# Maxima over partitions by products of ones, the table of exponentials first, first weights by halves, a new order

## The chip, the cores and the metric

The kernel runs on one NeuronCore of a Trainium2 chip. Its engines work side by side, each through its own queue in order: TensorE (PE, with its weight loads PEld), VectorE (DVE), ScalarE (ACT), GpSimd (POOL) and SyncE (SP), which here issues nearly all DMAs. The metric is device time in microseconds of one execution, lower is better.

## What is computed

Eight sequences of 576 positions go through attention with 8 heads of 64 and then through a feed-forward layer of width 2048 with a gate. Four heads see the last 32 positions, four see every fourth of the last 128.

```python
scores = scale * np.matmul(q, k.transpose(0, 1, 3, 2))
mask_plain = (rel >= 0) & (rel < window)                       # window = 32, heads 0 to 3
mask_dil = (rel >= 0) & (rel < window * dilation) & (rel % dilation == 0)   # dilation = 4, heads 4 to 7
scores = np.where(masks[None, :, :, :], scores, -1000000000.0)
attn = np.exp(scores - np.max(scores, axis=-1, keepdims=True))
attn = attn / (np.sum(attn, axis=-1, keepdims=True) + 1e-09)
x = np.matmul(attn, v)        # then (B, S, H * D)
h = x @ w_in
sp = np.where(h > 20.0, h, np.log1p(np.exp(np.minimum(h, 20.0))))
out = (h * np.tanh(sp)) @ w_out
```

The weights come as 64-bit floats, queries, keys and values as 32-bit floats.

## The kernel before

**Units.** The work is cut into 16 units u, half a sequence (288 positions) each. A unit passes through the attention of its four pairs of heads (pairs 0 and 1 plain, 2 and 3 dilated, whose positions are grouped by residue) and then through the feed-forward layer in four column groups j of 512.

**Numbers in two halves.** The feed-forward products run in float16 with each operand split into a high part and the rest (x, w, g), so one product becomes three. A split needs a scale, a power of two taken from the operand's largest magnitude. For the weights, `w_max`, `w_words`, `w_scale` and `w_split` turn the words of a 64-bit float into a float32 and split it; the maximum over partitions comes from a bf16 product with a matrix of ones (L349, L352), a sum over partitions, which is an upper bound of the maximum. A weight piece of 1 MB (two transfers of 512 KB, named wl k.g.p: which of w_in and w_out, group, half) goes through `w_max` on ACT (L338), a shift on DVE (L381) and two word steps on DVE (L383, L384) before the scale (L349 to L362) and the split (L393 on ACT, L396 on DVE). Four pieces have room at a time.

**`prep`** takes the maxima of a unit. Units 0 to 3 ("direct") do their attention in float32 and need only the maximum of v; unit 0 ("summed") takes sums of magnitudes by ACT (L461). Units 4 to 15 need maxima of q, k and v, reduced by DVE along the free axis (L291) into a tile m of 6 columns. Over the partitions they are joined in two ways:

- `over_partitions` (units 0 to 5): PE transposes m (L300), DVE reduces (L303) and, for six columns, spreads the result on a diagonal (L306), and a float32 product with ones (L309) brings it back to all partitions;
- from unit 6 on `partition_all_reduce` on POOL (L491).

DVE reads the result (L471, L494) and makes the scales from it (L285 to L287).

**What sets the order.** A text, `ORDER`, lists steps by name; each mention of a step lets its generator run up to the next `yield` and so issues that much to the engines' queues. A number behind = names the PSUM bank (there are four, "b") that the step takes. The names are: `ld`, `lv` loads of q and k and of v, `sp` score products (L594 for the mask, L597), `sc` their row maxima on DVE (L627), `ex` exponentials (for unit 0 PE subtracts the maxima, L649), `tp` transposes of probabilities (L716, copied by ACT L725), `va` products with v (L739 or L745, L753, L759, L760), `tx` transposes of x and their split (L787, L797, L800, L802), `ff` the first feed-forward product (L841) and Mish (L844), `gt` the gate's split, `fo` the second product (L872) and the output, `wl`, `wm`, `ww`, `ws`, `wp` the weights' steps, `pr` the steps of `prep`. `kw` followed by a number issues so many products of zeros (L901), the fillers; nobody reads them.

**The first instructions** stand outside the order: the identity and the masks are made by POOL (memsets, then selects; the identity's at masks.py:199), and ACT makes bf16 copies of both (L251, L253), which every score product of the direct units reads.

Of the kernel before, what the change touches and what calls it, by code (L numbers as in the profile page):

```python
# [42 lines left out]
wp0.0.0 wp0.0.0 kw16=0 kw8=0 va0.3=0 va0.3 tp0.0=3 tp0.0 va0.3 ex1.0 wp0.3.1 wl0.1.0 wm0.1.0 ww0.1.0 ww0.1.0 wl0.2.1
xa0 kw16=3 kw7=3 tx0.2=3 va0.0=1 tx0.2 kw15=2 tp1.0=2 kw16=0 kw10=0 tx0.2 tx0.2 tp1.0 va0.0 va0.0 tx0.3=0 kw13=3
va0.1=3 va0.1 tx0.3 va0.1 wl0.2.0 kw16=2 kw5=2 tx0.3 wm0.2.0 tx0.3 ex1.1 kw14=2 tx0.1=2 tx0.1 tx0.0=1 sp1.2=3 pr1
kw11=0 tx0.1 tx0.0 sp1.3=0 tx0.0 ww0.2.0 wl0.1.1 wm0.1.1 tx0.1 wm0.2.1 sc1.2 tx0.0 kw9=2 tp1.1=2 tp1.1 ex1.2 ww0.1.1
sc1.3 ex1.3 ww0.2.1 kw4=3 ws0.1=3 ws0.1 wp0.1.0 ld2 sp2.0=1 sc2.0 ex2.0 lv2 ws0.2=2 ws0.2 fs0 kw1=3 ff0.6=3 ff0.6
ff0.6 ff0.0=0 ff0.7=2 ff0.7 ww0.2.1 ff0.7 wp0.2.1 ww0.1.1 pr1=1 pr1 ff0.0 ff0.0 pr1 pr1 va1.0=3 va1.0 va1.0 va1.1=2
va1.1 va1.1 tp1.3=1 tp1.3 tp2.0=0 tp2.0 kw2=3 tx1.0=3 va1.3=1 va1.3 tx1.0 wp0.2.1 va1.3 pr2 tp1.2=2 tp1.2 wp0.1.1
wp0.1.1 tx1.1=0 tx1.1 tx1.1 kw12=2 va1.2=2 va1.2 va1.2 tx1.0 tx1.0 wp0.1.0 gt0.3=0 ff0.1=1 ff0.1 pr2=3 ff0.1 pr2 kw1=0  # L50
tx1.3=0 tx1.3 ww0.2.0 kw10=1 tx1.2=1 tx1.2 sp2.3=2 sc2.3 tx1.3 tx1.3 kw4=0 pr2 pr2 tx1.2 tx1.2 wl1.3.0 wm1.3.0 gt0.0=1
gt0.0 ww1.3.0 wp0.2.0 wp0.2.0 ww1.3.0 wl1.3.1 wm1.3.1 ww1.3.1 ww1.3.1 fs1 kw3=0 ff1.0=0 ff1.0 ff1.0 ff1.1=1 ff1.1
ff1.1 gt1.0=2 ff1.2=3 ff1.2 ff1.2 ff1.3=0 sp2.1=1 sc2.1 ws1.3=3 ws1.3 ff1.3 ex2.3 kw6=2 tp2.3=2 tp2.3 gt0.3 gt1.0
wl1.2.0 wm1.2.0 ww1.2.0 ww1.2.0 wl1.2.1 wm1.2.1 ww1.2.1 ww1.2.1 ex2.1 kw3=3 ff0.2=3 ff0.2 ff0.2 ff0.3=2 ff0.3 ff0.3
gt0.1=3 gt0.1 ff1.6=1 ff1.6 ws1.2=3 ff0.4=2 ff1.6 ws1.2 ff1.3 gt1.1=4 gt1.1 wp1.3.0 wp1.3.0 ff0.4 va2.3=1 ff0.4
tp2.1=0 tp2.1 va2.3 va2.3 wp1.2.1 wp1.2.1 ld3 sp3.0=3 sp3.1=2 lv3 sc3.0 sc3.1 ff1.7=0 ff1.7 ff1.7 gt1.3=5 gt1.3
wp1.2.0 wp1.2.0 wp1.3.1 wp1.3.1 wl1.0.1 wm1.0.1 ff1.4=1 ff1.5=0 ff1.5 ww1.0.1 ff1.4 ff1.4 ff1.5 gt1.2=6 gt1.2 wl1.0.0
wm1.0.0 ww1.0.0 ww1.0.0 va2.1=3 va2.1 va2.1 sp3.3=2 ff0.5=1 ff0.5 ff0.5 gt0.2=7 gt0.2 fo1.2.0=0 fo1.2.1 fo1.2.2
ws1.0=1 ws1.0 ex3.1 tp3.1=3 tp3.1 wl1.1.0 wm1.1.0 fo1.2.3 fo1.2.3 fo1.2.3 sc3.3 ex3.3 sp3.2=3 sc3.2 ex3.2 ww1.1.0
ww1.1.0 sp2.2=1 ld4 sc2.2 pr4 pr4 ex2.2 lv4 fo1.3.0 fo1.3.1 fo1.3.2 fo1.3.3 fo1.3.3 pr3 fo0.2.0=2 fo0.2.1 fo0.2.2  # L60
fo0.2.3 fs2 fo0.2.3 fo0.2.3 pr4 pr4 xa2 tx2.3=3 tx2.3 tx2.3 va2.0=1 tp2.2=0 tp2.2 va2.0 va2.0 wp1.0.0 ex3.0 wp1.0.0
fo0.3.0 fo0.3.1 fo0.3.2 fo0.3.3 fo0.3.3 pr4=0 ww1.0.1 fo1.3.3 pr4 fo0.3.3 tx2.0=3 va2.2=1 tx2.0 va2.2 tx2.0 kw2=2 pr4
# [897 lines left out]
```

## Time and profile before

| | |
|---|---|
| median of three runs | 922.4 us (921.63 to 923.58) |
| the profiled execution | 923.0 us, its span 921.1 us |
| granted TensorE clock | 1.00 of full speed |
| busy, of the span | PE 99%, weight loads 80%, DVE 64%, ACT 59%, POOL 2% |
| instructions of PE | 9422 products, 482 of them fillers |
| moved by DMA | 82.36 MB, 89 GB/s on average |

PE's busy time counts a product from its start to its modelled end, so fillers count as busy like any other. Idle time is written in brackets behind an instruction, with what ended it: "<-ACT pp" is a wait for ACT's writing of pp, "<-issue" is time for which the profile shows no reason. A row with xN is a group of N instructions.

### The profile page before, as it was taken

The page shows a single profiled execution, that of the slowest core. Times are in us where ns is not written, and L with a number is a line of the kernel's source. Part 1 is how long each engine was busy: PE and PEld are TensorE (multiplying, and loading weights), DVE is VectorE, ACT ScalarE, POOL GpSimd, SP SyncE. Part 2 cuts the span into 40 slices and gives each one's busy share as a digit, 9 for nine tenths or more (in the row PEclk, how much of TensorE's full clock was granted, in tenths as well). Part 3 has the DMA queues.
Part 4 walks back from the last instruction along what each step waited for, and adds up shares of the span by engine and source line. Part 5 has one row for each costly group of instructions (what it writes and reads, how often), then busy time and mean ns, then how long its engine had stood idle before and what let it go on. Part 6 is the DMA issues. An engine that isn't in the chain of part 4 may idle for free.

```text
span 921.1 us, 21816 instructions
## 1 busy us (share of the span) xinstructions
PE 911.5 (99%) x9422; PEld 738.0 (80%) x9422; DVE 593.1 (64%) x879; ACT 545.5 (59%) x804; POOL 22.0 (2%) x99
## 2 busy tenths in 40 slices
PE   9999999999999999999999999999999999999998
...
GB/s 292 217 117 139 140 139 105 56 105 16 119 81 110 69 106 95 98 62 103 102 100 96 100 72 113 72 55 120 52 33 119 87 55 59 36 41 35 20 14 27
DMA packets 156560, 82.36 MB, mean 89 GB/s; under 512 B 122960, under 2 KB 152368, under 8 KB 156464
## 3 DMA queue, kind: packets, MB, share of 16 engines
...
q8 instruction: 74, 1.21, 0.5%
...
## 4 chain that ended last, share of the span: by engine, by line
PE 99%; ACT 1%; issue 0%; DVE 0%; ACTq 0%
PE b L872 41%; PE b L841 41%; PE b L597 4%; PE b L745 3%; PE b L901 3%; PE b L739 2%; PE b L716 1%; PE b L594 1%; PE b L649 0%; PE b L352 0%; PE b L349 0%; PE b L800 0%; PE b L787 0%; ACT pp L725 0%; PE b L309 0%; ACT x L802 0%
## 5 line engine op out<-in xcount | busy, mean ns | idle before, releaser
L872 PE MATMUL b<-g,w 128*128 128x288 f16 x3072 | 388.1, 287 | 0.0
L841 PE MATMUL b<-x,w 128*128 128x288 f16 x3072 | 387.3, 286 | 0.0
L841 PEld LDWEIGHTS <-w 128*128 128x128 f16 x3072 | 297.6, 98 | 75.3
L872 PEld LDWEIGHTS <-w 128*128 128x128 f16 x3072 | 297.1, 98 | 75.4
L862 DVE SCALAR_TENSOR_TENSOR g<-hm,sg,g 128x1152 f16<-128x1152 f32 x64 | 89.8, 1414 | 116.8 <-ACT g L860 116.8
L844 ACT ACTIVATE hm<-b,fs 128x576 f32<-128x576 f32 x128 | 92.3, 737 | 102.4 <-PE b L841 88.4
L886 ACT ACTIVATE y<-b,fo 128x288 f32<-128x288 f32 x60 | 43.5, 724 | 126.6 <-PE b L872 116.5
L860 ACT ACTIVATE g<-hm,sg 128x1152 f16<-128x1152 f32 x64 | 79.9, 1253 | 3.2 <-PE b L872 1.6
L668 ACT ACTIVATE sb<-sb,ln_p 96x704 f32<-96x704 f32 (+3 forms) x48 | 42.4, 888 | 26.8 <-DVE sb L629 26.6
L629 DVE TENSOR_TENSOR sb<-sb,nm 72x576 f32<-72x576 f32 (+4 forms) x60 | 45.2, 754 | 2.1
L627 DVE TENSOR_REDUCE nm<-sb 72x8 f32<-72x576 f32 (+4 forms) x60 | 44.9, 748 | 1.7
L760 DVE TENSOR_TENSOR xs<-b,rec 72x512 f32<-72x512 f32 (+1 forms) x64 | 39.7, 620 | 6.5 <-DVE rec L759 0.5
...
L901 PE MATMUL b<-zeros 128*128 128x128 f16 x482 | 33.4, 229 | 5.1 <-ACT pp L725 2.1
L901 PEld LDWEIGHTS <-zeros 128*128 128x128 f16 x482 | 31.0, 103 | 7.3 <-issue 5.0
L759 DVE RECIPROCAL rec<-den 72x8 f32<-72x8 f32 (+1 forms) x64 | 12.0, 188 | 36.2 <-ACT den L755 27.3
L844 ACT ACT_TABLE_LOAD x22 | 28.2, 1283 | 9.1 <-PE b L841 8.7
L621 DVE SCALAR_TENSOR_TENSOR sb<-b,sc,m_r 96x704 f32<-96x704 f32 (+1 forms) x24 | 23.4, 976 | 15.3 <-PE b L597 6.3
L597 PEld LDWEIGHTS <-q 64*72 64x72 f16 (+1 forms) x1008 | 25.8, 116 | 8.3 <-issue 7.6
L597 PE MATMUL b<-k,q 64*72 64x72 f16 (+3 forms) x1008 | 30.9, 210 | 0.0
L621 DVE SCALAR_TENSOR_TENSOR sb<-b,sc,m_d 72x576 f32<-72x576 f32 (+1 forms) x24 | 22.6, 944 | 11.4 <-PE b L597 11.0
L521 DVE TENSOR_TENSOR q<-qn,q 128x288 f16<-128x288 f32 (+1 forms) x36 | 23.7, 708 | 7.2 <-ACT q L512 7.2
...
## 6 DMA issues: line engine op xcount, KB each, us to landing
qn<-in_qT SPq DMA_DIRECT2D x16, 576.0 KB
...
raw<-in_w_in SPq DMA_DIRECT2D x16, 512.0 KB
raw<-in_w_out SPq DMA_DIRECT2D x16, 512.0 KB
...
```

The lines of the kernel that those rows point to most:

```text
L597: nc.tensor.matmul(o, q, k, start=start, stop=stop, skip_group_check=True)
L621: nc.vector.scalar_tensor_tensor(args[0], args[1], d["sc"][:nq], args[2], ALU.mult, ALU.add)
L627: nc.vector.tensor_reduce(nm[:nq, :, j:j + n], x, axis=AX.X, op=ALU.max, negate=True)
L629: nc.vector.tensor_tensor(blocked(sb, c0, n, w), x, nm[:nq, :, j:j + n].unsqueeze(3).broadcast_to([nq, 2, n, w]), op=ALU.add)
L668: nc.scalar.activation(x, x, AF.Exp, bias=ln_p[:nq])
L841: nc.tensor.matmul(ph[:, h, :HT], w1[j][:, c, wi, k * P:(k + 1) * P], x_of(d, xi, c), start=(n == 0), stop=(n == len(seq) - 1))
L844: nc.scalar.activation(d["m"][j][:, k0:k0 + 2], ph[:, :, :HT], AF.Mish, scale=d["fs"][:, j:j + 1])
L860: nc.scalar.activation(g[:, 0], m, AF.Identity, scale=sg)
L862: nc.vector.scalar_tensor_tensor(g[:, 1], m, sg, g[:, 0], ALU.mult, ALU.subtract)
L872: nc.tensor.matmul(po[:, :HT], w2[:, e, j, wi, k * P:(k + 1) * P], d["g"][j][:, gi, k, :], start=(j == 0 and n == 0), stop=(j == NCH - 1 a ...
L886: nc.scalar.activation(o, src, AF.Identity, scale=fo)
L901: nc.tensor.matmul(warm[:, 1, 512 - P:], zeros, zeros, start=True, stop=True)
```

## The change

- `over_partitions` is now one bf16 product of a matrix of ones with the maxima, which m holds as bf16: a sum over partitions in place of the maximum, in all units from 1 to 15. The all-reduce on POOL is gone. Unit 0 keeps the transpose, the reduction and the float32 product under the name `top_of`.
- In `prep` of the direct units the two reductions over v stand in separate steps.
- At the very start, before the identity, ACT takes an exponential of a column of ones.
- For the first weight piece (0.3.0) `w_max` and `w_words` work on its two 512 KB blocks one after the other (`pieces`, `BY_BLOCK`).
- `ORDER` is another one. Fillers: 120 in place of 226 ahead of the first scores, 84 in place of 212 from there to the first feed-forward product, none in place of 44 after it. The steps of the first units, and of most later ones, stand in a new order, with other banks. The weight pieces and the loads of units are asked for in the same sequence.

```diff
 ORDER = """
-wl0.3.0 wl0.0.1 ld0 wm0.3.0 ww0.3.0 ww0.3.0 wm0.0.1 ww0.0.1 ww0.0.1 kw16=0 kw16=0 kw16=0 kw16=0 kw16=0 kw16=0 kw16=0
-kw16=0 kw16=0 kw16=0 kw16=0 kw16=0 kw16=0 kw16=0 kw2=0 sp0.0=0 sc0.0 sp0.1=1 sc0.1 wl0.0.0 wm0.0.0 ww0.0.0 sp0.3=2
-wl0.3.1 wm0.3.1 sp0.2=3 sc0.2 ex0.1 ex0.1 ex0.2 ex0.2 sc0.3 ex0.3 ww0.3.1 ww0.3.1 kw2=1 ws0.3=1 ws0.3 lv0 pr0 pr0
-kw16=3 kw16=3 kw7=3 pr0=3 pr0 ww0.0.0 wp0.3.0 tp0.2=1 xa1 ex0.3 ex0.0 tp0.2 pr0 pr0 tp0.1=2 tp0.1 ws0.0=1 ws0.0
...
+wl0.3.0 wl0.0.1 ld0 wm0.3.0 wm0.3.0 ww0.3.0 ww0.3.0 ww0.3.0 ww0.3.0 wm0.0.1 ww0.0.1 ww0.0.1 kw16=0 kw16=0 kw10=0
+kw16=0 kw16=0 kw16=0 kw16=0 kw14=0
+sp0.0=0 sc0.0 sp0.1=1 sc0.1 wl0.0.0 wm0.0.0 ww0.0.0 sp0.3=2 wl0.3.1 wm0.3.1 sp0.2=3 sc0.2 ex0.1 ex0.1 ex0.2 ex0.2
+sc0.3 ex0.3 ww0.3.1 ww0.3.1 ws0.3=1 lv0 pr0 pr0 ws0.3 kw16=3 kw8=3 pr0=3 pr0 ww0.0.0 wp0.3.0 tp0.2=1 ex0.0 xa1 ex0.3
...
@@
+BY_BLOCK = {(0, 3, 0)}
+
@@
+    ones = const.tile([P, 1], F32, name="ones")
+    nc.vector.memset(ones, 1.0)
+    warm = const.tile([P, 1], F32, name="warm")
+    nc.scalar.activation(warm, ones, AF.Exp)
     ident = const.tile([P, P], F32, name="ident")
     make_identity(nc, ident)
@@
     def over_partitions(m, n):
 
+        o = take("b", banks)[:, 0, :n]
+        nc.tensor.matmul(o, ones_b.broadcast_to([P, P]), m, start=True, stop=True)
+        yield
+        return o
+
+    def top_of(m, n):
+
         pm = take("b", banks)[:, 0]
-        nc.tensor.transpose(pm[:n, :P], m, ident)
-        yield
-        c = small.tile([8, 1], F32, name="c", bufs=4)
-        nc.vector.tensor_reduce(c[:n], pm[:n, :P], axis=AX.X, op=ALU.max)
-        if n > 1:
-            dg = small.tile([8, 8], F32, name="dg", bufs=2)
-            nc.vector.tensor_scalar(dg[:n, :n], ident[:n, :n], c[:n], None, ALU.mult)
-        yield
-        o = pm[:, 256:256 + n]
-        nc.tensor.matmul(o, ones[:n].broadcast_to([n, P]), dg[:n, :n] if n > 1 else c[:n], start=True, stop=True)
+        nc.tensor.transpose(pm[:1, :P], m, ident)
+        yield
+        c = small.tile([1, 1], F32, name="c", bufs=2)
+        nc.vector.tensor_reduce(c, pm[:1, :P], axis=AX.X, op=ALU.max)
+        yield
+        o = pm[:, 256:257]
+        nc.tensor.matmul(o, ones[:1].broadcast_to([1, P]), c, start=True, stop=True)
         yield
         return o
@@
+    def pieces(k, g, p):
+        return [slice(c, c + 1) for c in range(WIDE)] if (k, g, p) in BY_BLOCK else [slice(0, WIDE)]
+
     def w_max(k, g, p):
 
         _, hi = raws[k, g, p]
         a = w_dst(k, g, p).rearrange("p c a n -> p c (a n)").bitcast(F32)
-        nc.scalar.activation(a, hi.bitcast(F32), AF.Identity, scale=HI)
+        for c in pieces(k, g, p):
+            nc.scalar.activation(a[:, c], hi[:, c].bitcast(F32), AF.Identity, scale=HI)
+            yield
@@
-        nc.vector.tensor_scalar(a, a, 3, None, ALU.logical_shift_left)
-        yield
-        nc.vector.scalar_tensor_tensor(lo, lo, 29, a, ALU.logical_shift_right, ALU.bitwise_or)
-        nc.vector.scalar_tensor_tensor(lo, hi, -0x80000000, lo, ALU.bitwise_and, ALU.bitwise_or)
+        for c in pieces(k, g, p):
+            nc.vector.tensor_scalar(a[:, c], a[:, c], 3, None, ALU.logical_shift_left)
+            yield
+            nc.vector.scalar_tensor_tensor(lo[:, c], lo[:, c], 29, a[:, c], ALU.logical_shift_right, ALU.bitwise_or)
+            nc.vector.scalar_tensor_tensor(lo[:, c], hi[:, c], -0x80000000, lo[:, c], ALU.bitwise_and, ALU.bitwise_or)
+            yield
@@
-        m = pool.tile([P, 6], F32, name="m", bufs=3)
+        m = None if u in SUMMED else pool.tile([P, 6], BF16, name="m", bufs=3)
@@
-            o = yield from over_partitions(m[:, 0:1], 1)
+            o = yield from (top_of if u in SUMMED else over_partitions)(m[:, 0:1], 1)
@@
-        if u < FIRST + 3:
-            mr = yield from over_partitions(m, 6)
-        else:
-            mr = pool.tile([P, 6], F32, name="mru", bufs=2)
-            nc.gpsimd.partition_all_reduce(mr, m, P, bass_isa.ReduceOp.absmax)
-            yield
+        mr = yield from over_partitions(m, 6)
```

More of the change, by code (lines that the diff above doesn't have):

```diff
@@ L43 @@
[L43 to L62, printed above, removed]
@@ new lines @@
+sp2.3=2 sc2.3 tx1.3 tx1.3 pr2 tx1.2 tx1.2 wl1.3.0 wm1.3.0 ww1.3.0 gt0.0=1 gt0.0 wp0.2.0 wp0.2.0 ww1.3.0 wl1.3.1
+wm1.3.1 ww1.3.1 ww1.3.1 fs1 ff1.0=0 ff1.0 ff1.0 ff1.1=3 ff1.1 ff1.1 gt1.0=2 ff1.2=1 ff1.2 ff1.2 ff1.3=0 sp2.1=3
+ws1.3=1 ws1.3 ff1.3 sc2.1 ex2.3 tp2.3=1 tp2.3 gt0.3 gt1.0 wl1.2.0 wm1.2.0 ww1.2.0 ww1.2.0 wl1.2.1 wm1.2.1 ww1.2.1
+ww1.2.1 ex2.1 ff0.2=2 ff0.2 ff0.2 ff0.3=1 ff0.3 ff0.3 gt0.1=3 gt0.1 ff1.6=3 ff1.6 ff0.4=2 ws1.2=1 ff1.6 ws1.2 wp1.3.0
+ff1.3 gt1.1=4 gt1.1 ff0.4 ff0.4 va2.3=3 tp2.1=0 tp2.1 va2.3 va2.3 wp1.2.1 wp1.2.1 wp1.3.0 ld3 sp3.0=1 sp3.1=2 lv3
@@ new lines @@
+va4.3 va4.3 ex4.0 tp4.0=0 tp4.0 tp4.0=0 fo3.2.1 fo3.2.2 fo3.2.3 sc5.2 va4.1 va4.1 sp6.1=1 sc6.1 sp5.0=2 fo3.2.3
+fo3.3.0 xa4 tx4.1=1 tx4.1 va4.0=0 tx4.1 tx4.3=0 tx4.3 va4.2=1 va4.2 va4.0 va4.0 va4.2 tx4.3 ex5.2 tp5.2=2 tp5.2
+tp5.2=2 sc5.0 fo3.2.3 ex5.3 tp5.3=1 tp5.3 tp5.3=0 tx4.2=1 tx4.0=0 tx4.0 tx4.0 tx4.2 tx4.2 fo3.3.1 fo3.3.2 fo3.3.3
+fo3.3.3 fo3.3.3 sp6.3=0 sc6.3 fo3.0.0=1 fo3.0.1 fo3.0.2 fo3.0.3 fo3.0.3 va5.2=2 va5.2 sp6.2=3 va5.2 fo3.1.0 fo3.1.1
+va5.3=0 tp5.1=0 tp5.1 sc6.2 tp5.1=1 ex5.0 tp5.0=2 tp5.0 tp5.0=2 va5.3 va5.3 fo3.0.3 pr6 pr6 lv7 ex6.1 tp6.1=1 tp6.1
@@ new lines @@
+fo5.3.2 va7.1=0 va7.1 va7.1 tp8.0=1 tx7.1=0 tx7.1 tx7.1 fo5.3.3 fo5.3.3 pr9 pr9 gt6.0=2 fo5.1.1 fo5.1.2 fo5.1.3
+fo5.1.3 tp8.1=0 xa8 va7.0=2 va7.0 va7.0 tp8.3=0 ld10 pr10 ff6.6=0 ff6.6 ff6.6 pr10 pr10 gt6.0 va7.3=1 va7.3 va7.3
+tx7.0=1 tx7.0 tx7.0 pr9 pr9 ff6.4=3 ff6.5=2 ff6.5 ff6.5 lv10 fo5.3.3 ff6.4 ff6.4 gt6.2=0 gt6.2 tx7.3=0 va8.0=0 va8.0
+ff6.7=2 ff6.7 ff6.7 gt6.3=3 gt6.3 fo6.0.0=3 fo5.1.3 sp8.2=1 sc8.2 ex8.2 fo6.2.0=2 fo6.0.1 fo6.0.2 fo6.0.3 fo6.0.3
+tp8.1 fo6.0.3 tp8.1=2 sp9.2=1 fo6.2.1 fo6.2.2 sc9.2 tp8.2=2 tp8.2 sp9.1=1 sc9.1 tp8.2=1 fo6.2.3 fo6.1.0 fo6.1.1
@@ new lines @@
+fo8.3.3 fo8.3.3 fo8.3.3 ex11.3 tx9.3 va10.3=1 tp10.2=2 va10.3 va10.3 tx9.3 tx10.3=0 tx10.3 va10.0=2 va10.0 va10.0
+tp11.2 tp11.2=0 pr12 pr12 pr12 pr12 fo8.1.0 fo8.1.1 fo8.1.2 fo8.1.3 fo8.2.3 tx10.3 sp11.0=0 sc11.0 ex11.0 tp11.0=0
+tp11.0 fo8.1.3 fo8.1.3 ff9.2=1 ff9.3=2 ff9.3 ff9.3 ff9.2 ff9.2 gt9.1=0 gt9.1 ff9.6=0 ff9.7=3 ff9.7 ff9.7 va10.1=2
+va10.1 va10.1 tp11.0=1 ff9.6 ff9.6 tx10.0=1 tx10.0 tx10.0 va10.2=1 va10.2 va10.2 pr12 pr12 pr12 ld13 pr13 lv13
+tx10.2=0 tx10.2 va11.2=3 va11.2 va11.2 ff9.0=0 ff9.1=2 ff9.1 ff9.1 ff9.0 ff9.0 gt9.0=4 gt9.0 sp12.2=1 sc12.2 xa11
@@ L166 @@
+fo14.3.3 fo14.3.3 ff15.4 gt15.2=4 gt15.2 ff15.6=2 ff15.6 ff15.6 fo13.3.3 fo13.3.3 fo13.3.3 ff15.1=0 ff15.1 ff15.1
+gt15.0=2 gt15.0 ff15.3=3 ff15.3 ff15.3 gt15.1=1 gt15.1 ff15.7=2 ff15.7 ff15.7 gt15.3=3 gt15.3 fo15.2.0=1 fo15.0.0=0
+fo15.0.1 fo15.2.1 fo15.2.2 fo15.2.3 fo15.2.3 fo15.0.2 fo15.0.3 fo15.0.3 fo15.3.0 fo15.3.1 fo15.3.2 fo15.2.3 fo15.3.3
+fo15.3.3 fo15.0.3 fo15.3.3 fo15.1.0 fo15.1.1 fo15.1.2 fo15.1.3 fo15.1.3 fo15.1.3
 """.split()
```

206 lines of the change are left out of this document (100 added, 106 removed).

## The prediction

> **What bounds the kernel now.** I read the page first, then stages, then the stages that are not full of useful work, instruction by instruction.
>
> ```profile
> span 921.1 us, 21816 instructions
> PE 911.5 (99%) x9422; PEld 738.0 (80%) x9422; DVE 593.1 (64%) x879; ACT 545.5 (59%) x804; POOL 22.0 (2%) x99
> PE 99%; ACT 1%; issue 0%; DVE 0%; ACTq 0%
> L901 PE MATMUL b<-zeros 128*128 128x128 f16 x482 | 33.4, 229 | 5.1 <-ACT pp L725 2.1
> ```
>
> PE carries the chain from end to end, but 482 of its products multiply zeros (L901, the fillers, "kw" in the order). Table by stages (length, then busy time of PE, weight load, DVE, ACT, POOL; clock; DMA), all instructions, then the fillers alone:
>
> ```profile
> 1.04:16.29 15.25, 15.25 (x228) 15.22 (x228) 5.06 (x5) 4.34 (x6) 2.34 (x12) 1.00 0.96 336
> 16.29:25.00 8.71, 8.71 (x90) 5.86 (x88) 8.05 (x12) 5.01 (x7) 0.00 (x0) 1.00 1.01 262
> 25.00:59.27 34.27, 32.04 (x426) 27.32 (x424) 28.86 (x55) 24.36 (x48) 0.24 (x2) 1.00 0.71 204
> 59.27:160.80 101.53, 99.71 (x976) 81.67 (x974) 85.47 (x143) 70.53 (x131) 0.27 (x3) 1.00 0.38 118
> 160.80:896.00 735.20, 735.20 (x7548) 591.77 (x7546) 464.86 (x665) 438.20 (x611) 18.65 (x77) 1.00 0.33 75
> 896.00:921.10 25.10, 20.57 (x168) 16.18 (x166) 0.57 (x1) 3.10 (x4) 0.00 (x0) 1.00 0.07 25
> ...
> 1.04:16.29 15.25, 15.25 (x226) 15.08 (x226) 1.00 0.96 336
> ...
> 25.00:59.27 34.27, 13.60 (x211) 12.41 (x208) 1.00 0.71 204
> 59.27:160.80 101.53, 3.87 (x44) 3.04 (x43) 1.00 0.38 118
> ```
>
> From 160.80 to 896.00 PE never waits and has no filler to speak of: only a change of its own work counts there. All that can be won lies before 160.80: the fillers, and PE's waits of 34.27 - 32.04 = 2.23 us and 101.53 - 99.71 = 1.82 us. The tail after the last product stays.
>
> The start, in order of time (start, length, engine, line; in brackets the idle time before and what ended it):
>
> ```profile
> 6.08 1.28 ACT L338 ACT_TABLE_LOAD   x1 [6.08 <-DMA raw<-in_w_in]
> 7.37 1.15 ACT L338 ACTIVATE w<-raw 128x1024 f32<-128x1024 f32 x1
> 12.47 0.28 POOL masks.py:199 TENSOR_SCALAR_AFFINE_SELECT ident<-ident 128x128 f32<-128x128 f32 x1 [11.21 <-issue]
> 12.79 0.27 ACT L253 CAST ident_b<-ident 96x96 bf16<-96x96 f32 x1 [4.27 <-POOL ident masks.py:199]
> 13.18 1.13 ACT L338 ACTIVATE w<-raw 128x1024 f32<-128x1024 f32 x1
> 14.21 0.48 ACT L251 ACTIVATE m_fb<-m_f 96x352 bf16<-96x352 f32 x1
> 14.34 0.86 DVE L381 TENSOR_SCALAR w<-w 128x1024 int32<-128x1024 int32 x1 [2.58 <-ACT w L338]
> 16.34 1.18 ACT L338 ACTIVATE w<-raw 128x1024 f32<-128x1024 f32 x1 [1.64 <-DMA raw<-in_w_in]
> 19.02 1.16 ACT L338 ACTIVATE w<-raw 128x1024 f32<-128x1024 f32 x1 [1.51 <-DMA raw<-in_w_in]
> 20.70 1.42 DVE L627 TENSOR_REDUCE nm<-b 72x8 f32<-72x576 f32 x2 [0.52 <-PE b L597]
> 22.04 0.68 DVE L381 TENSOR_SCALAR w<-w 128x1024 int32<-128x1024 int32 x1
> 24.01 1.23 DVE L384 SCALAR_TENSOR_TENSOR raw<-raw 128x1024 int32<-128x1024 int32 x1
> ```
>
> Two things hold the start. POOL stands still for 11.21 us before its first select, with no instruction and no wait that the profile knows; the mask m_fb follows only at 14.69, and 226 fillers cover that. Behind it the DMA is full (0.96, then 1.01), and the third and fourth weight pieces come when it delivers them, at 16.34 and 19.02.
>
> **The change, part by part.** *Fillers.* Counted in the two order texts: 226 become 120 ahead of the first scores, 212 become 84 from there to the first feed-forward product, 44 become none after it; 278 fewer. Whether a filler's time comes back depends on who is late next, so each stage is asked by itself.
>
> *To 25 us.* The last all-reduce by POOL is removed. Nothing on the page says that the 11.21 us belong to it; yet the select that ends them takes 0.28 us, and beside memsets and copies POOL has but two kinds of work, selects at the start and all-reduces to the end. [...] The bounds are 0 (the stall stays) and 11.21 us (it goes); I take that it goes. The first weights by halves and the table load of 1.28 us moved ahead to idle time let ACT begin when the first half has come, before 6.08, instead of at 7.37, and ident_b no longer holds ACT for 4.27 us and with it DVE for 2.58. The first scores then wait for their keys:
>
> ```profile
> qn<-in_qT SPq DMA_DIRECT2D x16, 576.0 KB
> ...
> raw<-in_w_in SPq DMA_DIRECT2D x16, 512.0 KB
> ...
> knp<-in_kT SPq DMA_DIRECT2D x8, 288.0 KB
> ```
>
> Four weight transfers, the queries and the keys of the plain heads are 2.98 MB; at 336 GB/s that is 8.9 us, so they come at 9.9 us or somewhat later, near the end of 120 fillers (1.04 + 120 x 15.25/226 = 9.1 us). But none of this moves the fourth weight piece: ACT takes it at 19.02 in any case and ends at 20.18. Before, DVE then had the maxima of two score pairs (20.70 to 22.12) ahead of that piece's shift at 22.04 and ended its last word at 25.24. With the scores some 5 us earlier these maxima are over before 20.2, so the shift starts at 20.2: 1.8 us gained of the 7.2 us of fillers taken out. Bounds 0 and 3.
>
> *From 25 us to the first feed-forward product (59.27).*
>
> ```profile
> 26.66:57.33 30.67, 28.44 (x380) 24.52 (x377) 25.54 (x44) 21.57 (x38) 0.24 (x2) 1.00 0.72 215
> ...
> 42.64 0.83 ACT L797 CAST x<-b 128x288 f16<-128x288 f32 x1
> ...
> 44.15 1.62 PE L901 MATMUL b<-zeros 128*128 128x128 f16 x26
> ...
> 45.60 0.42 PE L800 MATMUL b<-x,minus 128*128 128x288 f16 x1
> ...
> 46.06 0.79 ACT L802 CAST x<-b 128x288 f16<-128x288 f32 x1 [2.58 <-PE b L800]
> ```
>
> The fillers here are not only padding of waits. The operand of the product at 45.60 was ready at 43.47; PE was busy with 26 fillers, and ACT waited 2.58 us for PE. So taking fillers out gains, until the next engine binds: 128 fillers at 13.60/211 = 64 ns are 8.2 us, which leaves PE some 24 us of the stage, while DVE has 25.54 us of work in 30.67. The same maxima, words and products remain for DVE, so the gain ends at its idle 5.13 us. Chains from PE over ACT to DVE and back remain; I take half, 2.5 us. Bounds 0 and 5.1.
>
> *From there to 160.80.* All 44 fillers go: 3.87 us. DVE has 85.47 of 101.53 us, so PE stays the bound; I count the fillers whole and leave the 1.82 us of waits as they are: 3.9 us. Bounds 0 and 5.7.
>
> *The maxima.* Rows of the old way on PE, of a product with the same stationary ones, of POOL's way, and of the reductions ahead of it:
>
> ```profile
> 27.01 0.27 PE L300 MATMUL b<-ident,m 128*1 128x128 f32 x1
> ...
> 28.95 0.38 PE L309 MATMUL b<-c,ones 1*128 1x1 f32 x2
> ...
> L491 POOL PARTITION_ALL_REDUCE mru<-m  x10 | 4.9, 486 | 311.4 <-DVE m L291 311.4
> ...
> L349 PEld LDWEIGHTS <-ones 128*128 128x128 bf16 x16 | 1.4, 97 | 1.1
> ...
> L291 DVE TENSOR_REDUCE m<-vn 128x1 f32<-128x768 f32 x15 | 14.1, 941 | 3.9 <-DMA vn<-in_v 3.9
> ...
> L291 DVE TENSOR_REDUCE m<-vdn 72x1 f32<-72x1024 f32 x7 | 8.5, 1208 | 1.6 <-DMA vdn<-in_vd 1.6
> ```
>
> Units 1 to 5 lose a transpose and a pair of float32 products (at most 0.27 + 0.38 = 0.65 us of PE each, at least the 0.38) and ten units lose an all-reduce of 0.49 us that cost PE nothing. All 15 get one bf16 product whose weight load is the 97 ns of L349; its few columns add little: 15 x 0.1 = 1.5 us against 5 x 0.4 = 2.0. Net 0.5 us gained, bounds 1.0 lost and 1.8 gained. POOL's memset of m stays, off the path.
>
> **Sum**, against the profiled execution's own time of 923.0 (span 921.1 and 1.9 around it): 923.0 - 1.8 - 2.5 - 3.9 - 0.5 = 914.3. That execution is 0.6 above the median of 922.4, so **913.7** for the median. All good ends together are 15.6 us (906.8), all poor ends a loss of 1.0; for this case by itself I take 907 to 919, the poor end being the fillers of the last stage alone, less 0.5.
>
> [...]
>
> **The rivals.** **A, every filler counts.** PE bears the chain, others wait for it, and its own waits inside the stages are 4.05 us only, so the 278 may be pure surplus: 7.2 + 8.2 + 3.9 + 0.5 = 19.8, so 903.2, or 902.6 as a median. Against: 19.02, and 25.54 us of DVE. **B, the stall stays.** The masks come at 14.69 as before, PE idles from 9.1, the maxima sit ahead of the shift again; only 2.5 + 3.9 + 0.5 remain: 915.5. For it: nothing in the trace ties the stall to the all-reduce. **D, the stall stays and PE's clock drops** in those 5.6 us: if the stage from 16.29 to 25.00 ran at half speed, 8.7 us more, 924.2. Against: all rows show clock 1.00; for: fillers kept every wait of PE short, so the trace cannot show it. [...]
>
> **C, slower: PE queues behind the maxima.** Before, units 6 to 15 had their maxima joined on POOL, which waited 311.4 us for DVE at nobody's cost. Now the joining product stands in PE's own queue, and all feed-forward products of other units queue behind it. If PE reaches it while the last two reductions still run (0.94 + 1.21 = 2.15 us) in each of units 4 to 15, that is 12 x 2.15 = 25.8 us: 939.5. It decides from 8.7/12 = 0.7 us per unit on. Against: DVE has 464.86 of 735.20 us there, so the reductions mostly run ahead of PE.
>
> **Chances.** Forecast 48%, A 17%, B 17%, D 5%, C 9%, and 4% that the new order loses elsewhere what it gains. The range holds the forecast's own, B and A: 902.5 to 920. Within 0.2% (1.8 us) is what a measurement of this kernel can't tell from no change. Faster: forecast, A, B and a rest of D and the last, 84%; same 6%; slower, C and half of D and of the last, 10%.
>
> **What would show it.** Right: POOL's first select before 2 us; first scores at 10 to 12 us; ACT's fourth weight piece still at 19.0; the first feed-forward product at about 55; DVE over 85% busy between 25 and 55; no wait of PE after 160 us; clock 1.00. Wrong: the first select near 12.5 (B, D); the first feed-forward product before 50 (A); PE waiting at the joining product after 160 us (C); or a wait of the first FFN stage that grows by what the fillers gave.

## The result, and the profile after

The changed kernel takes 914.29 us (median of 6 runs, 913.15 to 918.24), the kernel before, on the same chip, 922.06 (6 runs, 921.12 to 924.22): a ratio of 0.9917, 95% interval 0.9895 to 0.9939. Forecast were 913.7 and a range of 902.5 to 920. The profiled execution of the changed kernel took 913.45 us, its span 911.3.

The head of its page, and the chain that ended last (the granted clock in tenths; each digit is a fortieth of the span):

```profile
span 911.3 us, 21239 instructions
PE 897.5 (98%) x9144; PEld 723.6 (79%) x9144; DVE 590.1 (65%) x875; ACT 548.1 (60%) x808; POOL 17.3 (2%) x89
PEclk9899999999999999999999999999999999999999
PE 92%; DMA 3%; DVE 2%; ACT 1%; SPq 1%; issue 1%; DVEq 0%; ACTq 0%
```

278 products fewer on PE, as many as the fillers left out, and an 8 in the second slice of the clock, where the kernel before had nines throughout. PE is now 92% of the chain: DMA and VectorE have entered it.

The stages of the changed kernel, cut at its own first feed-forward product (53.80), and under them both kernels from their first feed-forward product to the end. Columns: length, busy time of PE, weight load, DVE, ACT, POOL, granted clock, DMA share, GB/s. The changed kernel first:

```profile
25.00:53.80 28.80, 25.84 (x268) 21.09 (x267) 26.01 (x46) 23.05 (x45) 0.24 (x2) 0.88 0.84 249
53.80:155.33 101.53, 100.20 (x968) 82.00 (x967) 87.10 (x154) 73.41 (x138) 0.27 (x3) 1.00 0.42 128
155.33:886.20 730.87, 730.15 (x7504) 587.25 (x7503) 460.42 (x649) 438.38 (x608) 13.95 (x67) 1.00 0.35 74
886.20:911.30 25.10, 21.36 (x175) 16.82 (x172) 1.36 (x1) 3.09 (x4) 0.00 (x0) 1.00 0.07 24
...
53.80:911.30 857.50, 851.71 (x8642) 686.06 (x8640) 548.88 (x803) 514.88 (x749) 14.21 (x70) 1.00 0.35 79
```

and the kernel before:

```profile
59.27:921.10 861.83, 855.49 (x8686) 689.62 (x8684) 550.90 (x807) 511.82 (x746) 18.93 (x80) 1.00 0.33 79
```

So the 9.8 us between the spans split in two: 59.27 - 53.80 = 5.47 us ahead of the first feed-forward product, 861.83 - 857.50 = 4.33 us behind it. The four terms of the sum had 1.8 + 2.5 = 4.3 and 3.9 + 0.5 = 4.4. The two profiled executions flatter the change: the one before lies above its median, the one after below, and the medians differ by 7.8 us only (6.9 in a second measurement, e10). The 8.7 us of the sum is somewhat more than either. Between 25 us and that product DVE is busy for 90% (26.01 of 28.80) and the clock is 0.88.

The start of the changed kernel, in order of time:

```profile
0.73 1.28 ACT L238 ACT_TABLE_LOAD   x1 [0.73 <-PEq L962]
1.30 0.29 POOL masks.py:199 TENSOR_SCALAR_AFFINE_SELECT ident<-ident 128x128 f32<-128x128 f32 x1
4.87 0.69 ACT L351 ACTIVATE w<-raw 128x512 f32<-128x512 f32 x1 [2.64 <-DMA raw<-in_w_in]
10.12 0.50 ACT L256 ACTIVATE m_fb<-m_f 96x352 bf16<-96x352 f32 x1
12.88 0.85 PE L610 MATMUL b<-knp,qn 64*96 64x128 f32 x12 [1.75 <-DMA knp<-in_kT]
19.18 1.12 ACT L351 ACTIVATE w<-raw 128x1024 f32<-128x1024 f32 x1 [1.53 <-DMA raw<-in_w_in]
20.33 0.69 DVE L396 TENSOR_SCALAR w<-w 128x1024 int32<-128x1024 int32 x1 [0.63 <-ACT w L351]
22.32 1.23 DVE L399 SCALAR_TENSOR_TENSOR raw<-raw 128x1024 int32<-128x1024 int32 x1
```

POOL's first select stands at 1.30 us, with nothing ahead of it: the 11.21 us have gone. The fourth weight piece is still taken at 19.18 (19.02 before), its shift on DVE begins at 20.33 instead of 22.04, its last word step ends at 23.55 instead of 25.24. The first scores wait 1.75 us for their keys.

What was not foreseen stands on PE a little later. Instructions of PE, and two stretches with the columns of the stages:

```profile
33.47 1.25 PE L752 MATMUL b<-vdn,pp 72*72 72x65 f32 x16 [0.93 <-ACT pp L738]
36.40 0.71 PE L800 MATMUL b<-ident,xs 72*128 72x72 f32 x4 [1.17 <-ACT sb L675]
39.77 2.44 PE L914 MATMUL b<-zeros 128*128 128x128 f16 x21
44.41 0.67 PE L914 MATMUL b<-zeros 128*128 128x128 f16 x9
...
32.35:35.76 3.41, 1.95 (x26) 1.58 (x23) 3.24 (x7) 3.22 (x7) 0.00 (x0) 0.96 0.90 305
35.76:42.59 6.83, 6.19 (x48) 6.16 (x48) 6.66 (x9) 3.75 (x11) 0.00 (x0) 0.52 0.92 313
```

At 39.77 a filler takes 2.44/21 = 116 ns, at 44.41 it takes 74: PE ran at half clock for 6.83 us, after 3.41 us in which it was busy for 57%, though no single wait there was longer than 1.17 us. (The last section has these two stretches with the exact moments at which the clock changes.)

### The profile page after: what moved, and what is told of

The parts are those of the page before. It is cut to its first block, busy times and chain, and to the rows that moved or that the text cites. A ratio compares the mean times of both kernels' runs of the same rounds, so it can differ in the third digit from the quotient of the medians.

```text
span 911.3 us, 21239 instructions
## 1 busy us (share of the span) xinstructions
PE 897.5 (98%) x9144; PEld 723.6 (79%) x9144; DVE 590.1 (65%) x875; ACT 548.1 (60%) x808; POOL 17.3 (2%) x89
## 4 chain that ended last, share of the span: by engine, by line
PE 92%; DMA 3%; DVE 2%; ACT 1%; SPq 1%; issue 1%; DVEq 0%; ACTq 0%
PE b L885 41%; PE b L854 39%; PE b L610 4%; PE b L758 3%; DMA raw<-in_w_in 2%; PE b L752 1%; PE b L729 1%; DMA knd<-in_kdT 1%; PE b L914 0%; DVE m L296 0%; PE b L366 0%; SPq L332 0%; ACT w L409 0%; PE b L607 0%; DMA vdn<-in_vd 0%
## 5 line engine op out<-in xcount | busy, mean ns | idle before, releaser
L681 ACT ACTIVATE sb<-sb,ln_p 72x576 f32<-72x576 f32 (+3 forms) x48 | 42.5, 889 | 24.0 <-DVE sb L642 23.8
L642 DVE TENSOR_TENSOR sb<-sb,nm 96x512 f32<-96x512 f32 (+4 forms) x60 | 45.2, 754 | 2.1
L640 DVE TENSOR_REDUCE nm<-sb 96x4 f32<-96x512 f32 (+4 forms) x60 | 44.9, 748 | 1.6
L719 DVE TENSOR_TENSOR p<-sb,p 72x576 f16<-72x576 f32 (+3 forms) x34 | 30.2, 887 | 9.4 <-ACT p L717 9.4
L610 PE MATMUL b<-k,q 64*96 64x128 f16 (+3 forms) x1008 | 31.3, 210 | 0.0
L717 ACT CAST p<-sb 72x576 f16<-72x576 f32 (+3 forms) x34 | 26.5, 781 | 0.7
L351 ACT ACTIVATE w<-raw 128x1024 f32<-128x1024 f32 (+1 forms) x17 | 18.6, 1101 | 12.6 <-DMA raw<-in_w_in 12.6
```

What stands on the lines that cost most here:

```text
L610: nc.tensor.matmul(o, q, k, start=start, stop=stop, skip_group_check=True)
L640: nc.vector.tensor_reduce(nm[:nq, :, j:j + n], x, axis=AX.X, op=ALU.max, negate=True)
L642: nc.vector.tensor_tensor(blocked(sb, c0, n, w), x, nm[:nq, :, j:j + n].unsqueeze(3).broadcast_to([nq, 2, n, w]), op=ALU.add)
L681: nc.scalar.activation(x, x, AF.Exp, bias=ln_p[:nq])
```

## The experiments

The theory after the result: the stall belongs to the all-reduce; ahead of the first feed-forward product the gain is whatever VectorE and the DMA leave of the fillers taken out; behind it each filler comes back; and fillers do a second thing, they hold PE's clock (0.88 between 25 us and that product in the changed kernel, 1.00 in the kernel before). Rivals: the stall alone was the cost; the fillers were surplus everywhere; the halves and the early table load brought the gain.

Every profiled execution divides at the first feed-forward product. The table gives where that product starts, the length from there to the end of the span, the clock of that execution, and the timed runs beside it:

| kernel | first feed-forward product | from there to the end | clock | median us (runs) | ratio to before, 95% |
|---|---|---|---|---|---|
| before | 59.27 | 861.83 | 1.000 | 922.06 (6) | |
| after | 53.80 | 857.50 | 0.996 | 914.29 (6) | 0.9917 [0.9895, 0.9939] |
| e1_fill_226 | 56.42 | 857.08 | 0.993 | 915.37 (4) | 0.9925 [0.9912, 0.9938] |
| e2_pool_joins | 58.52 | 856.88 | 0.990 | 921.67 (12) | 0.9990 [0.9977, 1.0004] |
| e3_start_fillers_only | 56.70 | 856.50 | 0.989 | 917.98 (12) | 0.9965 [0.9942, 0.9988] |
| e4_gap_fillers | 54.82 | 856.48 | 0.996 | 913.53 (4) | 0.9906 [0.9894, 0.9919] |
| e5_gaps_filled | 53.34 | 858.46 | 0.999 | 913.08 (4) | 0.9897 [0.9885, 0.9910] |
| e6_before_no_join | 58.47 | 861.23 | 1.000 | 922.28 (11) | 0.9996 [0.9988, 1.0005] |
| e7_before_start_fillers_only | 55.55 | 858.25 | 0.992 | 918.67 (12) | 0.9964 [0.9949, 0.9979] |
| e8_no_halves_no_table | 55.00 | 856.70 | 0.994 | 913.97 (4) | 0.9906 [0.9893, 0.9919] |
| e9_no_late_fillers | 59.81 | 858.29 | 0.999 | 918.59 (5) | 0.9963 [0.9950, 0.9975] |
| e10_after_again | 55.46 | 857.44 | 0.993 | 915.19 (5) | 0.9925 [0.9912, 0.9937] |
| e11_gaps_filled_a | 58.69 | 856.51 | 0.993 | 912.81 (5) | 0.9896 [0.9880, 0.9911] |
| e12_gaps_filled_b | 53.38 | 856.62 | 1.000 | 913.10 (5) | 0.9901 [0.9884, 0.9917] |

The kernel before, run beside them, had medians of 922.25 (e1 to e4), 922.36 (e5 to e8) and 922.04 (e9 to e12); each ratio is against its own. Read the third column first: behind that product there are two levels, 861 to 862 with the 44 late fillers of before and 856.5 to 858.5 without them. All the rest of the difference lies ahead of it, and so does the scatter, as far as two executions of the changed kernel tell: they differ by 1.66 us ahead of that product and by 0.06 behind it. The profiled execution of e2 is one of its two fastest (917.22; ten of the twelve runs took 920.97 to 924.09 at a lower clock), and that of e11 is its slowest (917.41).

### The stall: e6 and e2

Two kernels settle whose the stall is. In the kernel before, the all-reduce left out (each partition keeps its own maxima, so the joining over partitions isn't computed for units 6 to 15):

```diff
-            mr = pool.tile([P, 6], F32, name="mru", bufs=2)
-            nc.gpsimd.partition_all_reduce(mr, m, P, bass_isa.ReduceOp.absmax)
+            mr = m
```

> The kernel before with the all-reduce of GpSimd left out and nothing in its place: units 6 to 15 take their scales from each partition's own maxima, the joining over partitions is not computed. Theory 1 (the stall at the start belongs to the all-reduce): the first select is at 1.3 us, ident_b no longer holds ACT, the second weight piece is taken when it lands, at 9 us, but the first scores still stand behind 226 fillers at 16.1 us, so the time is the same within 1 us, 921.5 to 922.5 us. Theory 2 (the stall has another cause): the select stays at 12.5 us. Theory 3 (the early start of DVE is what gains): 920 us or less.

In the changed kernel, the all-reduce put back for units 6 to 15:

```diff
-        m = None if u in SUMMED else pool.tile([P, 6], BF16, name="m", bufs=3)
+        by_pool = u >= FIRST + 3
+        m = None if u in SUMMED else pool.tile([P, 6], F32 if by_pool else BF16, name="mp" if by_pool else "m", bufs=3)
@@
-        mr = yield from over_partitions(m, 6)
+        if not by_pool:
+            mr = yield from over_partitions(m, 6)
+        else:
+            mr = pool.tile([P, 6], F32, name="mru", bufs=2)
+            nc.gpsimd.partition_all_reduce(mr, m, P, bass_isa.ReduceOp.absmax)
+            yield
```

> The changed kernel with the all-reduce on GpSimd put back for units 6 to 15 (float32 maxima there), the order unchanged. Theory 1 (the stall of 11.2 us before the first select belongs to the all-reduce at the end of the execution before): the first select is at about 12.5 us again, the masks at about 14.7, PE waits some 5 us from 9.7 us on, the clock may fall there, and the time is 1.8 us (stall alone) to 6 us (with a clock at half) longer: 916 to 920 us. Theory 2 (the stall went for another reason, for instance the exponential at the start or the order of the first instructions): the first select stays at 1.3 us and the time stays within 1 us, at 914 us.

The first select in the kernel before without its all-reduce, with ACT's copy of the mask and the first scores:

```profile
1.30 0.29 POOL masks.py:199 TENSOR_SCALAR_AFFINE_SELECT ident<-ident 128x128 f32<-128x128 f32 x1
10.51 0.50 ACT L251 ACTIVATE m_fb<-m_f 96x352 bf16<-96x352 f32 x1
15.72 0.85 PE L596 MATMUL b<-knp,qn 64*96 64x128 f32 x12
```

and in the changed kernel with the all-reduce back, with its stages of 2 us:

```profile
12.85 0.28 POOL masks.py:199 TENSOR_SCALAR_AFFINE_SELECT ident<-ident 128x128 f32<-128x128 f32 x1 [11.59 <-issue]
15.10 0.74 PE L613 MATMUL b<-m_fb,ident_b 96*96 96x352 bf16 x2 [4.83 <-ACT m_fb L256]
...
10.00:12.00 2.00, 0.28 (x5) 0.10 (x2) 0.00 (x0) 0.00 (x0) 0.00 (x0) 1.00 1.14 346
12.00:14.00 2.00, 0.00 (x0) 0.15 (x1) 0.00 (x0) 0.83 (x3) 1.15 (x7) 0.71 1.06 407
14.00:16.00 2.00, 0.90 (x4) 0.38 (x5) 1.27 (x2) 1.15 (x3) 0.97 (x5) 0.50 1.03 422
16.00:18.00 2.00, 2.00 (x16) 1.31 (x16) 1.97 (x2) 1.07 (x1) 0.00 (x0) 0.50 1.15 311
18.00:20.00 2.00, 2.00 (x19) 1.52 (x20) 1.49 (x4) 1.12 (x1) 0.00 (x0) 0.58 0.76 141
```

The stall comes and goes with the all-reduce, in both orders, though the first all-reduce comes at about 240 us. Yet its removal from the kernel before is worth nothing that the runs can tell (922.28, ratio 0.9996): there 226 fillers stand ahead of the scores, which come at 15.72 in place of 16.52. In the changed kernel its return costs 921.67 - 914.29 = 7.4 us in the median, nearly the whole gain. The trace shows PE waiting 4.83 us for the mask and then working at half clock until 20 us, and again from 40 to 50 us; but it is one of the two runs at 917, some 3 us above the changed kernel's median, at a mean clock of 0.990. The other ten have 0.981 to 0.985, so more half clock than this trace shows; where it lies there, no trace tells. Ahead of the first feed-forward product, neither the stall's removal nor the new order with its fewer fillers gains without the other. Behind the first feed-forward product the joining on POOL is neither dearer nor cheaper: 856.88 against 857.50.

### The fillers of the start, the halves, the table: e1 and e8

The changed kernel with 226 fillers ahead of the first scores, as before:

```diff
 kw16=0 kw16=0 kw16=0 kw16=0 kw14=0
+kw16=0 kw16=0 kw16=0 kw16=0 kw16=0 kw16=0 kw10=0
```

> The changed kernel with 226 fillers ahead of the first scores, as before the change, and nothing else. Theory 1 (the start is bound by the weight transfers, the fourth piece is taken at 19.2 us whatever PE does): the first scores move from 12.9 to about 16.1-16.5 us, their maxima on DVE fall in front of the fourth piece's shift again, which goes from 20.3 back to about 22 us; the loss is about 1.8 us, so 916 us. Theory 2 (every filler counts): 106 fillers of 67 ns are 7.1 us, less the 3.2 us that PE waits at the start of the changed kernel, so 918 us or more. A third outcome, equal or faster, would say that the early scores are worth nothing and that a fuller PE keeps its clock up.

915.37 us: 1.1 above the changed kernel, 0.2 above its second measurement (e10, 915.19). The shift of the fourth weight piece, in its trace:

```profile
20.93 0.68 DVE L397 TENSOR_SCALAR w<-w 128x1024 int32<-128x1024 int32 x1
```

That is 0.60 later than the 20.33 of the changed kernel. Some 7 us of fillers are thus worth 0.2 to 1.1 us in the medians, less than the 1.8 us of the forecast, and the runs cannot tell that from nothing. In e6, where only the stall is gone from the kernel before, the shift begins at 21.23. So of the 1.7 us by which it comes sooner, 0.8 came with the stall's going, 0.3 with what else differs in e1, and 0.6 with the 106 fillers.

Without the halves of the first weights and without the early table load:

```diff
-BY_BLOCK = {(0, 3, 0)}
+BY_BLOCK = set()
@@
-    warm = const.tile([P, 1], F32, name="warm")
-    nc.scalar.activation(warm, ones, AF.Exp)
```

> The changed kernel without two of its parts: the first weight piece goes through ACT and DVE as a whole, and the table of exponentials is loaded where the first activation stands. Theory 1 (both fall into time in which ACT and DVE wait for DMA): ACT takes the first piece at about 7.4 us in place of 4.9, DVE ends its words at about 11.8 in place of 9.3, the fourth piece is still taken at 19.2, and the time is the same within 1 us, 914 us. Theory 2 (the early start counts): 1.3 to 2.5 us slower, 916 us.

913.97 us, inside the runs of the changed kernel. In this kernel the mask's copy on ACT begins at 10.48 (10.12 with both edits) and the first scores come at 11.75, before those of the changed kernel's profiled execution. The two edits are worth nothing that these runs can tell: the shift of the fourth piece begins at 20.25 without them and at 20.33 with them.

### The late fillers: e9

The kernel before without the 43 fillers behind its first feed-forward product (the 44th stands in the order right ahead of that product and stays):

```diff
-va1.1 va1.1 tp1.3=1 tp1.3 tp2.0=0 tp2.0 kw2=3 tx1.0=3 va1.3=1 ...
+va1.1 va1.1 tp1.3=1 tp1.3 tp2.0=0 tp2.0 tx1.0=3 va1.3=1 ...
...
```

> The kernel before with one edit: the 43 fillers behind its first feed-forward product are left out (kw2=3, kw12=2, kw1=0, kw10=1, kw4=0, kw3=0, kw6=2, kw3=3, kw2=2). Nothing else is changed. Theory 1 (the term of the forecast: from the first feed-forward product on PE is the bound, a filler taken out there comes back whole): 3.8 us less than the kernel before, 918.2 us, PE's idle time behind that product no longer than the 6.3 us of before, granted clock 1.00. Theory 2 (the fillers covered waits of PE there): PE's idle time behind that product grows by most of 3.8 us and the time is 921 to 922 us. Theory 3 (they held the clock): a stretch at half clock behind the first feed-forward product and 919 to 922 us.

From its first feed-forward product to the end:

```profile
59.81:918.10 858.29, 853.27 (x8643) 687.71 (x8641) 551.04 (x807) 511.85 (x746) 18.94 (x80) 1.00 0.34 79
```

861.83 - 858.29 = 3.5 us of the 3.8 expected, and 922.04 - 918.59 = 3.5 us in the medians. The fillers do come back. But not as the row of their busy time has it: PE's busy time falls by 855.49 - 853.27 = 2.2 us only, and its idle time falls too, from 6.34 to 5.02. The changed kernel goes on from there to 851.71 busy and 5.79 idle: 858.29 - 857.50 = 0.8 us for the maxima, the new order behind that product and the 44th filler, where 0.5 was the term for the maxima. These are single executions; those of the nine rows with the changed kernel's program behind that product (all but before, e2, e6, e7 and e9) spread from 856.48 to 858.46, so the 0.8 is not resolved.

### No fillers at all: e3 and e7

The changed kernel with its 84 later fillers out, and the kernel before with its 256 later ones out; those ahead of the first scores stay in both:

```diff
-sc0.3 ex0.3 ww0.3.1 ww0.3.1 ws0.3=1 lv0 pr0 pr0 ws0.3 kw16=3 kw8=3 pr0=3 pr0 ww0.0.0 ...
+sc0.3 ex0.3 ww0.3.1 ww0.3.1 ws0.3=1 lv0 pr0 pr0 ws0.3 pr0=3 pr0 ww0.0.0 ...
...
```

> The changed kernel with the 84 fillers after the first scores left out, the 120 at the start kept. Theory 1 (from 32 us on these fillers cost nothing to the chain, which runs over ACT and DVE, but hold the granted clock): the clock is at half for two or more windows in place of the 6.8 us seen, its mean falls from 0.996 to 0.99 or less, and the time is the same or up to 4 us longer, 914 to 918 us. Theory 2 (fillers are time that comes back): 84 x 64 ns = 5.4 us faster, 909 us.

> The kernel before with its 256 fillers after the first scores left out, its order otherwise unchanged. Theory 1 (fillers hold PE back where ACT and DVE wait for it, but without any the clock falls): PE's time comes back only in part, the mean clock falls to 0.98 or so, and the time is between 914 and 921 us, scattered. Theory 2 (every filler counts): 256 x 66 ns = 17 us faster, 905 us. Theory 3 (the new order and not the fillers brings the gain): the same as before within 2 us, with clock 1.00.

The changed kernel gets slower without them, 917.98 against 914.29 (and 915.19 in e10), and eleven of its runs spread from 913.12 to 925.66, longer with a lower clock (0.991 to 0.972); the twelfth took 927.63 at 0.970. Two stretches of its trace at half clock, the first of them with the stretch ahead of it:

```profile
21.00:25.00 4.00, 2.12 (x15) 0.91 (x14) 3.83 (x8) 2.68 (x6) 0.00 (x0) 1.00 0.90 271
25.00:33.00 8.00, 8.00 (x41) 5.29 (x38) 5.51 (x16) 3.81 (x6) 0.00 (x0) 0.57 0.68 147
39.11:52.77 13.66, 12.16 (x78) 9.82 (x79) 11.84 (x18) 11.29 (x22) 0.24 (x2) 0.50 0.96 309
```

The kernel before gains 922.36 - 918.67 = 3.7 us by the same edit, hardly more than the 3.5 that e9 gains by the 43 late fillers alone. Its 213 other fillers, and there are 13.6 us of them, bring next to nothing by themselves in the median: what their going frees, a lower clock seems to take back (its runs are longer with a lower clock, from 915.6 at 0.992 to 923.37 at 0.983). That this part of the gain needs the new order is argued, not shown: e7 has the stall too, and no run takes these fillers out of the old order with the stall gone.

### Fillers where PE waits: e4, e5, and e10 to e12

If the half clock of the changed kernel costs time on the path, fillers in PE's waits should win it back. The smallest edit first, then one with 10 more behind sp0.2 and some ahead of pr0 and tp0.0:

```diff
 kw16=0 kw16=0 kw16=0 kw16=0 kw14=0
+kw16=0 kw16=0
@@
-va0.2=1 tp0.3=0 tp0.3 va0.2 va0.2
+va0.2=1 tp0.3=0 kw12=1 tp0.3 va0.2 va0.2
```

> The changed kernel with 44 fillers more, in places where PE waits anyway: 32 ahead of the first scores (PE waits there from 9.7 us for the masks and to 12.9 us for the keys) and 12 behind the transposes of unit 0's pair 3 (PE waits 0.93 us at 32.6 us). Theory 1 (the half clock from 35.8 to 42.5 us comes of a window in which PE was busy 57% of the time, and the products done at half clock are on the chain): the clock stays at 1.00 there, the first feed-forward product comes 2 to 3 us before 53.6, and the time is about 912 us. Theory 2 (the clock falls for another reason, or ACT and DVE bind there in any case): the time stays at 914 us, or goes up by the fillers' 0.8 us.

```diff
-sp0.2=3 sc0.2
+sp0.2=3 kw10=3 sc0.2
@@
-ws0.3 kw16=3 kw8=3 pr0=3 pr0
+ws0.3 kw16=3 kw16=3 kw2=3 pr0=3 kw5=3 pr0
@@
-va0.3=0 tp0.0=3 va0.3 tp0.0
+va0.3=0 tp0.0=3 va0.3 kw16=0 tp0.0
```

> The changed kernel with fillers in all the places before 37 us where PE waits for something that comes no sooner: the 44 of the run with gap fillers, and 10 behind the fourth score pair (18 us), 10 more ahead of the maximum of v (23 us), 5 behind its transpose (24 us), 16 behind the transposes of pair 0 (35 us). Theory 1 (the clock falls to half for windows of 3.4 us after a stretch in which PE was busy about 75% of the time or less, and the half clock lies on the chain): the mean clock is 0.998 or more, the first feed-forward product comes at about 51 us, the runs lie closer together, and the time is 911 to 912 us. Theory 2 (ACT and DVE bind, so the clock is without effect there): the time stays at 913.5 to 914.3 us with whatever clock.

The second has the edits of the first as well. Its ten fillers behind sp0.2 go to the bank that holds unit 0's scores of pair 2 and change them; the work is otherwise the same. 913.53 and 913.08: each better than the changed kernel in the median, neither apart from it by its interval. In the second the clock was 1.00, 1.00, 0.999 and 0.996, yet two runs of it took 912.2, not the 911 to 912 hoped for. A busy share of 75% is no limit in these runs: e4 fell to half clock at the end of 4.00 us in which PE was busy for 2.97 (23 to 27 us), but kernel b below kept 1.00 with PE busy for 1.50 of 3.40 us (39.50 to 42.90).

So the changed kernel was run once more beside two kernels without those ten fillers, a (e11) with the other edits between 25 and 50 us alone, b (e12) with the 32 ahead of the scores too. The edits of a add 10 + 5 + 12 + 16 = 43 fillers, not the 39 of the text for a:

> The changed kernel itself once more, unchanged, beside the runs sent with it. Both theories expect 914.3 us, between 913.1 and 915.5, with a granted clock of 0.993 to 0.997 over the span; the gain over the kernel before 0.8%.

> The changed kernel with 39 more fillers between 25 and 50 us: kw8=3 becomes kw16=3 kw2=3 ahead of pr0=3, kw5=3 behind it, kw12=1 ahead of tp0.3, kw16=0 ahead of tp0.0. They stand where PE waited. The fillers ahead of the first scores stay 120. Theory 1 (the half clock between 35 and 43 us costs time on the path): the granted clock stays at 1.00 there, the first feed-forward product comes half a us to one us earlier than in the changed kernel, 913.0 us. Theory 2 (that stretch is bound by VectorE, PE's clock there is free): the clock stays at 1.00 and the time is that of the changed kernel within 0.4 us. Theory 3 (fillers cost what they take): the first feed-forward product comes 1 to 2 us later, 915 to 916 us.

> As the run before this one, and with 32 more fillers ahead of the first scores (152 in place of 120). Theory 1: clock 1.00 throughout the first 60 us, 913.0 us. Theory 2: the time of the changed kernel within 0.4 us. Theory 3: 1 us more than the run before this one, since the first scores stand behind 32 products more.

912.81 and 913.10 against 915.19: 2.4 and 2.1 us (1.5 and 1.2 against the first six runs' 914.29), and the intervals of a and of the changed kernel just part (0.9880 to 0.9911, 0.9912 to 0.9937). Those of b, and of the changed kernel's first six runs, overlap. Both kernels are better than before by 1%, and probably better than the changed kernel by 0.2%; the runs with the clock at 1.00 took 911.38 to 913.26. The clock isn't safe in them either. In the profiled execution of a, PE was idle for most of 10 to 14 us and then ran at half clock until 28, though it was busy throughout, and the first feed-forward product came at 58.69; that run took 917.41:

```profile
10.00:14.00 4.00, 0.96 (x11) 0.66 (x12) 3.15 (x3) 1.10 (x2) 0.00 (x0) 1.00 1.10 367
14.00:28.00 14.00, 14.00 (x79) 8.41 (x76) 7.23 (x11) 5.61 (x8) 0.00 (x0) 0.51 0.95 258
```

Kernel b, whose 32 fillers stand in that gap, kept 1.00 through its profiled execution, with the first feed-forward product at 53.38:

```profile
0.00:53.38 53.38, 47.52 (x579) 39.07 (x580) 41.26 (x73) 33.29 (x61) 3.09 (x19) 1.00 0.87 266
```

53.38 against 53.80: a whole clock wins 0.4 us over the changed kernel's better execution, and 2.1 us over the one of e10 (55.46), which spent two stretches at half clock:

```profile
19.50:26.20 6.70, 6.70 (x33) 4.08 (x32) 4.56 (x10) 4.14 (x8) 0.00 (x0) 0.50 0.87 241
36.70:43.30 6.60, 5.75 (x43) 5.44 (x42) 6.32 (x10) 4.33 (x12) 0.00 (x0) 0.50 0.96 340
```

Which engine is late in this stage changes with the clock. Pieces of the chain that ended last, traced back from the first feed-forward product (start, length, engine, tile, line); first the changed kernel, in part at half clock, where the chain runs on PE from 36.40 on but for 0.8 us of ACT, and 4.5 us of it are fillers (L914):

```profile
37.11 1.91 PE b L752 x12
39.01 0.96 PE b L729 x6
39.97 2.24 PE b L914 x21
```

and kernel b at full clock, where the view has it run over VectorE from 28.32 to 50.80, with one DMA transfer of weights in between:

```profile
34.09 0.88 DVE nm L641
39.36 5.98 DMA raw<-in_w_in
45.35 2.07 DVE m L297 x2
```

That the whole clock gains only 0.4 us over the changed kernel's better execution fits this: VectorE stands close behind PE.

## Why the prediction was right, and where it was not

**The start (1.8 us): right in the trace; its worth in the total is not shown.** That the stall goes with the all-reduce was a choice between two bounds, which no row of before showed; e6 and e2 show it (first select at 1.30 and at 12.85). The fourth weight piece at 19.0 held as the limit, the shift came at 20.33 (20.2 forecast), and the piece's last word step ended 25.24 - 23.55 = 1.7 us earlier. The first scores came at 12.88, not at 10 to 12, since the keys did; in e8 and e10 they came at 11.75 and 11.68, and the shift came at 20.25 and 20.14, hardly sooner. But e6 has 0.8 us of the 1.7 and no shorter time, and e1 loses 0.6 of it for 0.2 to 1.1 us.

**From 25 us to the first feed-forward product (2.5 us): inside its bounds, with luck in the size.** 5.47 - 1.7 = 3.8 us in the profiled execution; in e10, whose word step ended at 23.36, 59.27 - 55.46 - 1.9 = 1.9 us. The step had DVE bind and took half of its idle 5.13 us, a choice between two bounds. DVE is busy for 90% in the changed kernel, but the chain above runs on PE there, at half clock, and over DVE only in kernel b at full clock. So the limit that the step names holds at the clock that it assumed. That the clock is what moves the term between 1.9 and 3.8 fits one stretch of half clock in the one trace and two in the other; two traces do not prove it.

**Behind it (3.9 and 0.5 us): the fillers right, the maxima not resolved.** e9 gives 3.5 for 43 of the 44 fillers. The 0.8 that remains for the maxima and the order is smaller than the scatter; e2, with POOL joining again, has 856.88 there against 857.50 and 857.44.

**The clock at 1.00: wrong.** This is the step that failed, and the one place where the prediction named the loss and put it aside. Rival D had fillers covering the clock, but only for the case that the stall stays, at 5%. The stall went, and PE still lost its clock (0.50 for 6.83 us in the changed kernel), at waits of about 1 us, for which the sum had no term. The price is some 1.2 to 2.4 us in the median (e11 and e12 against the two measurements of the changed kernel) and most of the spread: the runs of the changed kernel lengthen from 913.15 to 918.24 as their clock falls from 0.996 to 0.986. So the nearness of 914.29 to the forecast 913.7 is in part luck: a loss that the sum lacks stands against a stage that gave more than its term, and the second measurement, 915.19, lies 1.5 us off.

**The rivals.** A, every filler counts: the first feed-forward product would have come before 50; it came at 53.80, and e3, with still fewer fillers, was slower. B and D, the stall stays: the select at 1.30 decides against them, but e2, which makes the stall stay, took 921.67, between B's 915.5 and D's 924.2, with the half clock that D had (0.50 from 14 to 18 us). C, PE queues behind the maxima: the waits of PE behind 160 us, whole, in the changed kernel (total, times, longest):

```profile
PE b L303 <- DVE m L296: 0.5, 1, 0.5
PE b L885 <- ACT hm L857: 0.2, 1, 0.2
```

One wait of 0.5 us at one joining product of twelve, where 2.15 us in each was C's price. The products themselves, and the rows of the old way, to read the 0.5 us term by (ns least, median, most):

```profile
L303 PE MATMUL b<-m,ones x15: 166/168/180, 62.6 to 703.5; 128*128 128x6 bf16 x12, 128*128 128x1 bf16 x3
```

```profile
L300 PE MATMUL b<-ident,m x6: 273/273/276, 27.0 to 220.2; 128*1 128x128 f32 x4, 128*6 128x128 f32 x2
L309 PE MATMUL b<-c,ones x8: 245/256/267, 28.9 to 163.8; 1*128 1x1 f32 x8
```

A joining product takes 168 ns, not the 100 assumed, so 15 of them are 2.5 us of PE's records instead of 1.5. By the same records the old way took 273 + 2 x 256 ns = 0.79 us in each of five units, 3.9 us. Records of PE overlap (two of 256 ns stand in 0.38 us in the prediction's row), so neither sum is time on the path, and no run has the joining products of units 1 to 5 alone.

The gap ahead of POOL's first select hangs on whether the program has the all-reduce: 11.21 us in the kernel before and 11.59 in e2 with it, none in the changed kernel and in e6, whose Pool work is selects, memsets and copies and whose first select stands at 1.30.
